# Another set of per-stage settings for the order of a fused attention and MLP kernel, without GpSimd's waits on the shared port

## The chip, the cores and the metric

The kernel runs on one core of one Trainium2 chip. The metric is the device time of one execution in microseconds, the median of three runs. Where the profile is spoken of, times are those of one profiled execution, and its span runs from the first to the last instruction of the program.

Engine names in the profile: PE is TensorE's matmul, PEld its weight load, DVE is VectorE, ACT is ScalarE, POOL is GpSimd, SP is SyncE, which issues most of the DMAs.

## The reference, cut to what matters

The input x has 2,048 rows of 512 numbers in bfloat16. Two branches work on it and a gate, one number per row, mixes them.

```python
def _A_ref(x, wqkv, wo):                       # attention: H = 32 heads of Dh = 16
    qkv = (x @ wqkv).reshape(B, S, 3, H, Dh).transpose(2, 0, 3, 1, 4)
    q, k, v = qkv[0], qkv[1], qkv[2]
    scores = jnp.einsum("bhqd,bhkd->bhqk", q, k) * (Dh ** -0.5)
    p = _softmax(scores, axis=-1)
    o = jnp.einsum("bhqk,bhkd->bhqd", p, v)
    return o.transpose(0, 2, 1, 3).reshape(B, S, D) @ wo

def _B_ref(x, w1, w2, w3, w4):                 # mixer: layernorm, w1, gelu, shifts by 1 and 2 rows, w2
    ...
    x1 = x + hs
    h2 = _gelu(_layernorm(x1, axis=-1) @ w3) @ w4   # MLP, F = 1792
    return x1 + h2

g = _sigmoid((x * gate_w).sum(-1, keepdims=True))
return g * a + (1 - g) * b
```

With 32 heads, 2,048 queries and 2,048 keys, the scores are 32 x 4 x 16 = 2,048 tiles of 128 keys x 512 queries. Each has to be exponentiated. That is the greatest part of the work.

## The kernel before

**How a score tile becomes probabilities.** There are two ways. ScalarE takes two tiles at once out of PSUM (psA), applies the exponential and writes bfloat16 into a PA buffer; each tile then needs one matmul with V, which adds into acc. VectorE takes one tile at a time (from a bank called ring), and computes the bits of a power of two directly: one multiplication and one addition, written as a 16-bit integer that is read as bfloat16. To make the approximation smooth, four copies of that integer, each shifted by a further constant, are all multiplied with V (two of them with a scaled V2) and added up. So a VectorE tile costs one first pass, a share of three shifted copies (made for two tiles at once, a pair), and four matmuls with V.

```python
def p1():                                        # VectorE, first pass, one tile
    nc.vector.tensor_scalar(out=pr["buf"].slot[:, h * 512:(h + 1) * 512], in0=buf.slot[:], scalar1=BITS_MUL,
                            scalar2=BITS_ADD, op0=ALU.mult, op1=ALU.add)
```

Who makes the three shifted copies k = 1, 2, 3 of a pair is decided when the pair is closed, by two settings and the urgency:

```python
def close_pair(pr):
    evs["n"] = evs.get("n", 0.0) + K.GP2         # every time the sum reaches 1: copy 2 too on GpSimd
    both = evs["n"] >= 1.0
    if both:
        evs["n"] -= 1.0
    rl = pr["pv"][0][0]
    alone = n_left(rl) <= (K.URG_L if rl == NR - 1 else K.URG)
    evs["m"] = evs.get("m", 0.0) + 1.0 - K.GP3   # every time the sum reaches 1: all three on VectorE
    if evs["m"] >= 1.0:
        evs["m"] -= 1.0
        alone = True
    both = both and not alone
    ...
    for k in range(1, 4):
        def sh(k=k):
            d = [b.slot for b in bufs]
            if alone or k == 1 or k == 2 and not both:
                return nc.vector.tensor_scalar(out=d[k][:, 0:w], in0=d[0][:, 0:w], scalar1=float(SHIFT * k), ...)
            return nc.gpsimd.tensor_scalar(out=d[k][:, 0:w], in0=d[0 if both else 2][:, 0:w], scalar1=1.0,
                                           scalar2=float(SHIFT * (k if both else 1)), op0=ALU.mult, op1=ALU.add)
        if alone or k == 1 or k == 2 and not both:
            j = dve(..., pr["jobs"], sh, prio=K.S_PRIO, acq=[bufs[k]], frees=[bufs[0]], port=True)
        else:
            j = gp(..., pr["jobs"] if both else last, sh, prio=1, acq=[bufs[k]], ...)   # gp() sets port=True
        ...
```

So in the ordinary case VectorE makes copies 1 and 2 from the first one, and GpSimd makes copy 3 from copy 2. There are 12 PD buffers for these integers.

**How the order comes about.** When the program is built, a small model of the engines (the class Sim) plays the whole kernel through with assumed durations and decides what each engine does next. The instructions are then issued in the order of the model's times; on the chip each engine works through its own list in that order, and semaphores keep the data right. The model treats a VectorE job and a GpSimd job that are both marked `port=True` as excluding each other:

```python
if any(not self.free[b.cls] for b in j.acq) or j.port and self.lock > self.t:
    continue
...
self.emit(self.t, self.in_port_order(e, j.fn) if j.port else j.fn)
self.t_free[e] = self.t + j.hold
if j.port:
    self.lock = self.t + j.hold
```

The kernel before carries that order over to the chip in one direction: each GpSimd instruction of such a job waits for the last VectorE instruction marked `port` that precedes it in the plan.

```python
def in_port_order(self, e, fn):
    def issue():
        inst = fn()
        if e == "DVE":
            self.last_port = inst
        elif inst is not None and self.last_port is not None:
            self.tc.add_manual_dep(inst.ins, self.last_port.ins.name, ..., reason="port")
    return issue
```

**The settings.** The model's choices depend on some two dozen settings, K. They have defaults (BASE), and for each stage of 32 score tiles (SEG = 32, so 64 stages) some of them are replaced:

```python
BASE = dict(P1_PRIO=0.414, S_PRIO=0.38, GP2=0.0, GP3=1.0, DVE_STOP=6, DVE_STOP_L=8, URG=5, URG_L=17, DVE_ALONE=2,
            EARLY=68, SL=(45, 60), IDLE_NS=537, PD_LOW=0, PA_LOW=0, DVE_WAIT=3, AHEAD=9, AHEAD2=9, PV_FULL=0.916,
            PV_IDLE=0.37, PRESS=27, MAXU=9, ROT=0, DUE_SH=0, AT_SH=0)
...
def pe_pick():
    t = sim.t
    if sim.tiles // SEG != stage[0]:
        stage[0] = sim.tiles // SEG
        K.__dict__.update({**BASE, **STAGES.get(stage[0], {})})
```

GP2 and GP3 share out the shifted copies as shown. P1_PRIO and S_PRIO rank VectorE's first passes and shifted copies. AHEAD and AHEAD2 say how far tiles of the next round may be taken early; a round is 64 tiles, one head from each of four groups, that add into acc together. DVE_ALONE and DVE_WAIT say when VectorE may be given a tile and how many may wait for it. PV_FULL, PV_IDLE, PRESS, SL, IDLE_NS and MAXU decide how many matmuls with V, and of the projections and the MLP, go between two batches of score matmuls. EARLY, AT_SH and DUE_SH shift when projections and MLP may or must run.

When a round's 64 tiles are done, VectorE copies acc out (accsb), its sums go through DRAM, are inverted and multiplied by the gate, come back broadcast (bcs), and GpSimd multiplies both into oT; this GpSimd instruction is marked `port` too, as are those of the layernorm (rs).

Of the kernel before, what the change touches and what calls it, by code (L numbers as in the profile page):

```python
# [11 lines left out]
ALU = mybir.AluOpType  # L12
# [7 lines left out]
SHIFT = 32  # L20
# [69 lines left out]
class Sim:  # L90
# [47 lines left out]
            self.n += 1  # L138
            self.order.append((t, self.n, fn))

    def in_port_order(self, e, fn):

        def issue():
            inst = fn()
            if e == "DVE":
                self.last_port = inst
            elif inst is not None and self.last_port is not None:
                self.tc.add_manual_dep(inst.ins, self.last_port.ins.name, mybir.DependencyInfo(
                    mybir.DependencyClass.Sync, mybir.DependencyReason.DATA), reason="port")
        return issue  # L150

    def finish_job(self, job):
        job.done = self.t
        self.release(job.frees)
# [1 line left out]
    def try_engine(self, e):  # L156
        if self.t_free[e] > self.t:
            return False
        best = None
        for j in self.jobs[e]:  # L160
            if j.at > self.tiles:
                continue
            if j.ready is None:
                if any(d.done is None for d in j.deps):
                    continue
                j.ready = self.t
            if any(not self.free[b.cls] for b in j.acq) or j.port and self.lock > self.t:
                continue
            key = (j.prio, j.ready, j.seq)
            if best is None or key < best[0]:  # L170
                best = (key, j)
        if best is None:
            return False
        j = best[1]
        self.jobs[e].remove(j)
        for b in j.acq:
            self.take(b)
        j.start = self.t
        self.emit(self.t, self.in_port_order(e, j.fn) if j.port else j.fn)
        self.t_free[e] = self.t + j.hold  # L180
        if j.port:
            self.lock = self.t + j.hold
        self.busy[e] += j.hold
        self.log.append((e, self.t, j.hold, j.name))
        self.push(self.t + j.hold, None)
        self.pending -= 1
        self.push(self.t + j.hold + j.lat, lambda: self.finish_job(j))
        return True
# [57 lines left out]
def kernel(  # L246
# [14 lines left out]
    nc = tc.nc  # L261
# [35 lines left out]
        P1_PRIO=0.414,  # L297
        S_PRIO=0.38,
        GP2=0.0,
        GP3=1.0,  # L300
        DVE_STOP=6,
        DVE_STOP_L=8,
        URG=5,
        URG_L=17,
        DVE_ALONE=2,
        EARLY=68,
        SL=(45, 60),
        IDLE_NS=537,
        PD_LOW=0,
        PA_LOW=0,  # L310
        DVE_WAIT=3,
        AHEAD=9,
        AHEAD2=9,
        PV_FULL=0.916,
        PV_IDLE=0.37,
# [2 lines left out]
        ROT=0, DUE_SH=0, AT_SH=0,  # L318
    )
    SEG = 32  # L320
    STAGES = {0: {'AHEAD': 6, 'EARLY': 13, 'DVE_ALONE': 150, 'S_PRIO': 0.368}, 1: {'AHEAD': 8, 'S_PRIO': 0.415}, 2: {'ROT': 3, 'URG': 3, 'MAXU': 9, 'PD_LOW': 3}, 3: {'PA_LOW': 3, 'DVE_WAIT': 4}, 4: {'SL': (25, 60), 'URG': 2, 'DVE_STOP_L': 9, 'DUE_SH': 40}, 5: {'SL': (25, 60), 'URG': 2, 'DVE_STOP_L': 9, 'DUE_SH': 40}, 6: {'S_PRIO': 0.234}, 7: {'PRESS': 17, 'DVE_WAIT': 5}, 8: {'PV_FULL': 0.776, 'AHEAD': 7, 'PD_LOW': 0}, 9: {'PV_FULL': 0.877, 'ROT': 2, 'AHEAD': 6, 'PA_LOW': 0}, 10: {'PV_FULL': 0.794, 'PA_LOW': 0, 'SL': (165, 60), 'DVE_ALONE': 2}, 11: {'SL': (85, 100), 'EARLY': 62}, 12: {'EARLY': 124, 'PV_IDLE': 0.433, 'DVE_STOP_L': 11, 'SL': (25, 40)}, 13: {'GP3': 0.6, 'DVE_ALONE': 150}, 14: {'ROT': 3, 'GP3': 0.9, 'URG_L': 16, 'AHEAD2': 12}, 15: {'P1_PRIO': 0.309, 'DVE_STOP_L': 5, 'AT_SH': 60, 'DVE_STOP': 5}, 16: {'DVE_WAIT': 2, 'AHEAD2': 10}, 17: {'ROT': 1, 'AT_SH': 10, 'GP3': 0.8, 'DVE_ALONE': 2}, 18: {'P1_PRIO': 0.403, 'GP2': 0.2}, 19: {'PRESS': 10}, 20: {'URG': 7, 'AT_SH': 60, 'GP2': 0.2}, 21: {'IDLE_NS': 352, 'DVE_ALONE': 300}, 22: {'S_PRIO': 0.257}, 23: {'PRESS': 52, 'AT_SH': 60}, 24: {'PA_LOW': 3, 'PRESS': 23, 'GP3': 0.8}, 25: {'PV_IDLE': 0.414, 'AT_SH': 10}, 26: {'DUE_SH': 8, 'PD_LOW': 1, 'GP2': 0.2, 'GP3': 0.9}, 28: {'AHEAD2': 10, 'EARLY': 142}, 29: {'AHEAD': 8, 'S_PRIO': 0.388, 'GP3': 0.9, 'ROT': 1}, 30: {'PV_IDLE': 0.372, 'DUE_SH': -40, 'S_PRIO': 0.412, 'PA_LOW': 2}, 31: {'IDLE_NS': 311, 'GP3': 0.9, 'P1_PRIO': 0.22}, 32: {'DUE_SH': 40, 'DVE_STOP': 5}, 33: {'DVE_STOP_L': 7, 'SL': (205, 60)}, 34: {'P1_PRIO': 0.326, 'PD_LOW': 0, 'PV_IDLE': 0.37, 'GP2': 0.35}, 36: {'PD_LOW': 1, 'DVE_STOP': 7}, 37: {'URG': 4, 'IDLE_NS': 589}, 38: {'ROT': 2}, 39: {'EARLY': 155, 'PA_LOW': 3}, 40: {'DUE_SH': -20, 'PRESS': 8}, 41: {'P1_PRIO': 0.584, 'PA_LOW': 3, 'MAXU': 10}, 42: {'AHEAD2': 8, 'PRESS': 58, 'DVE_ALONE': 0}, 43: {'PD_LOW': 0, 'DVE_WAIT': 2, 'P1_PRIO': 0.216, 'PV_FULL': 1}, 44: {'MAXU': 7, 'ROT': 1}, 45: {'PRESS': 10, 'SL': (65, 80)}, 46: {'DVE_WAIT': 6, 'AT_SH': 120, 'PD_LOW': 0}, 47: {'DUE_SH': 80, 'P1_PRIO': 0.59, 'DVE_ALONE': 150, 'AHEAD2': 6}, 48: {'URG': 8, 'AT_SH': 120}, 49: {'PD_LOW': 3, 'ROT': 3, 'DVE_WAIT': 6, 'AT_SH': 120}, 50: {'DVE_WAIT': 1, 'SL': (5, 60), 'GP2': 0.35, 'DVE_STOP_L': 11}, 51: {'PA_LOW': 3, 'URG_L': 18}, 52: {'ROT': 2, 'PD_LOW': 1, 'PRESS': 35}, 53: {'URG_L': 16, 'IDLE_NS': 245, 'PRESS': 19}, 54: {'PD_LOW': 3}, 56: {'MAXU': 10, 'GP2': 0.1}, 57: {'URG': 2}, 58: {'ROT': 3, 'DVE_WAIT': 5}, 59: {'ROT': 1}, 60: {'GP2': 0.2, 'PV_FULL': 0.879, 'SL': (85, 100)}, 61: {'GP3': 0.6, 'GP2': 0.35, 'PV_FULL': 0.985}, 62: {'GP3': 0.6, 'GP2': 0.35, 'PV_FULL': 0.985}}
    K = SimpleNamespace(**BASE)


# [70 lines left out]
        "den": slots("den", 3, [4, 512], F32, dpool),  # L395
        "rr": slots("rr", 3, [4, 512], F32, dpool),
    })
    sim.tc = tc
    sim.last_port = None

    def dve(hold, deps, fn, **kw):
        return sim.add(Job("DVE", hold, 280.0, deps, fn, **kw))
# [558 lines left out]
    def close_pair(pr):  # L961
        evs["pair"] = None
        evs["n"] = evs.get("n", 0.0) + K.GP2
# [5 lines that stand above are left out]
        evs["m"] = evs.get("m", 0.0) + 1.0 - K.GP3  # L969
# [4 lines that stand above are left out]
        w = 512 * pr["h"]  # L974
        bufs = [pr["buf"]] + [Buf("PD", pr["h"] + (k == 2)) for k in range(1, 4)]
        pr["buf"].users = pr["h"] + (3 if both or alone else 2)
        bufs[2].users = pr["h"] + (0 if both or alone else 1)
        last = list(pr["jobs"])
        chain = [last]
        for k in range(1, 4):  # L980
            def sh(k=k):
                d = [b.slot for b in bufs]
                if alone or k == 1 or k == 2 and not both:
                    return nc.vector.tensor_scalar(out=d[k][:, 0:w], in0=d[0][:, 0:w], scalar1=float(SHIFT * k),  # L984
                                                   scalar2=None, op0=ALU.add)
                return nc.gpsimd.tensor_scalar(out=d[k][:, 0:w], in0=d[0 if both else 2][:, 0:w], scalar1=1.0,  # L986
                                               scalar2=float(SHIFT * (k if both else 1)), op0=ALU.mult, op1=ALU.add)
            if alone or k == 1 or k == 2 and not both:
                j = dve(0.26 * w + 72.0, pr["jobs"], sh, prio=K.S_PRIO, acq=[bufs[k]], frees=[bufs[0]], port=True)
            else:  # L990
                j = gp(0.833 * w + 165.0, pr["jobs"] if both else last, sh, prio=1, acq=[bufs[k]],
                       frees=[bufs[0 if both else 2]])
            if k == 3:
                j.frees.append(pr["token"])
            last = [j]
            chain.append(last)
        for h2, (r2, kt2, i2, G2, p2) in enumerate(pr["pv"]):
            for k in range(4):
                hd = 8 * G2 + 2 * i2 + p2
                V = (lambda kt=kt2, hd=hd: V0[:, kt, hd, :]) if k < 2 else (lambda kt=kt2, hd=hd: V2[:, kt // 2, hd, :])  # L1000
                add_pv(r2, i2, kt2, V, lambda h2=h2, b=bufs[k]: b.slot[:, h2 * 512:(h2 + 1) * 512].bitcast(BF16),
                       list(chain[k]) + [j_v[kt2, G2 // 2] if k < 2 else j_v2[kt2, G2 // 2]], bufs[k])
# [371 lines left out]
```

The softmax here doesn't subtract the row's maximum and nothing guards it: scores larger than these inputs give would overflow.

## Time and profile before

| what | value |
|---|---|
| time, median of 3 runs (lowest to highest) | 772.39 us (772.31 to 772.64) |
| span of the profiled execution | 770.4 us, at a granted TensorE clock of 1.00 |
| instructions | 23,725 |
| score tiles on ScalarE, on VectorE | 1,483 and 565 |
| shifted copies on VectorE, on GpSimd | 579 and 270 |

In the profile's groups a row names the line, engine and operation, what is written and read, the shapes and the count; then the busy time and the mean duration of one; then how long the engine was idle just before such instructions, and what ended most of that idle time. A mean longer than busy time divided by the count says that neighbours overlap: the exponential shows a mean of 1,052 ns, but 742 of them fill only 689.8 us. In the list of waits a row gives who waited, for whom, the total, the number of times and the longest, in us. The line numbers: L922 is the exponential, L948 VectorE's first pass, L984 and L986 the shifted copies on VectorE and GpSimd, L842 the score matmul, L1017 the matmul with V, L532 the projections and the MLP, L1050 GpSimd's oT, L603, L623, L695 and L753 other VectorE instructions marked `port`, L684 the layernorm's on GpSimd.

### The profile page before, as it was taken

Reading aid. Unit: us, or ns where it says so; the run is one execution under the profiler, and the core shown is the slowest. Engines: PE = TensorE matmul, PEld = TensorE weight load, DVE = VectorE, ACT = ScalarE, POOL = GpSimd, SP = SyncE. Lnnn points to the kernel's source line nnn. Section 1 sums busy time; section 2 is a strip of 40 time slices with the busy share of each in tenths; the row PEclk is TensorE's granted clock in tenths of the full one; section 3 lists DMA queues with packets and bytes.
Section 4 is the critical chain, followed back from the end, with each engine's and each line's share of the span. In section 5 each row is a group of like instructions: output and inputs, shape, how many; then the busy total and the mean of one; then the engine's idle time right before and its main releaser. Section 6 shows DMA issues by size and latency. Waiting matters only on the chain.

```text
span 770.4 us, 23725 instructions
## 1 busy us (share of the span) xinstructions
PE 758.7 (98%) x9588; PEld 227.8 (30%) x9588; DVE 725.2 (94%) x1575; ACT 739.7 (96%) x767; POOL 335.2 (44%) x332
## 2 busy tenths in 40 slices
PE   9999999999999999999999999999999999999997
PEld 5333322223222222233232224222233222223222
DVE  6999999999999999998989998999999889999996
ACT  6899999999999999999989999999999999999995
POOL 2345533443344444344345553344454454454531
PEclk9999999999999999999999999999999999999999
DMA  9402133122001221141001001001100000000001
GB/s 192 142 3 35 54 98 88 47 72 89 6 19 34 61 72 46 48 125 50 17 18 33 23 20 47 23 27 27 41 19 19 23 19 22 27 20 20 13 18 38
DMA packets 67093, 34.60 MB, mean 45 GB/s; under 512 B 46748, under 2 KB 62380, under 8 KB 66984
## 3 DMA queue, kind: packets, MB, share of 16 engines
q1 hardware_dynamic: 66040, 32.56, 16.3%
q8 instruction: 75, 1.23, 0.6%
q10 hardware_dynamic: 944, 0.52, 0.2%
q14 instruction: 34, 0.28, 0.1%
HBM read 17.40 MB, written 6.81 MB: 31 GB/s over the span
## 4 chain that ended last, share of the span: by engine, by line
PE 71%; ACT 22%; DVE 4%; issue 3%; ACTq 0%; DVEq 0%
PE acc L1017 26%; PE psA L842 23%; PE ring L532 20%; ACT PA L922 16%; DVE PD L948 2%; ACT hT L766 2%; ACT hB L766 2%; DVE PD L984 1%; ACT hT L735 1%; ACT L922 1%; PE ring L842 1%; PE ring L510 0%; ACT L766 0%; PE ring L1295 0%; DVE hB L765 0%
## 5 line engine op out<-in xcount | busy, mean ns | idle before, releaser
L922 ACT ACTIVATE PA<-psA 128x1024 bf16<-128x1024 f32 x742 | 689.8, 1052 | 16.8 <-PE acc L1017 7.7
L986 POOL TENSOR_SCALAR PD<-PD 128x1024 uint16<-128x1024 uint16 x270 | 281.8, 1048 | 384.7 <-DVE PD L984 215.8
L948 DVE TENSOR_SCALAR PD<-ring 128x512 uint16<-128x512 f32 x565 | 372.9, 680 | 25.9 <-PE ring L842 23.6
L1017 PE MATMUL acc<-PD,V 128*17 128x512 bf16 x2260 | 307.3, 381 | 1.0 <-DVE accsb L1033 0.8
L842 PE MATMUL psA<-q,kT 32*128 32x512 bf16 x1483 | 285.8, 384 | 5.3 <-ACT PA L922 4.4
L1017 PE MATMUL acc<-PA,V 128*17 128x512 bf16 x1483 | 277.6, 381 | 0.0
L984 DVE TENSOR_SCALAR PD<-PD 128x1024 uint16<-128x1024 uint16 x579 | 226.2, 429 | 1.5 <-PE acc L1017 0.8
L842 PE MATMUL ring<-q,kT 32*128 32x512 bf16 x565 | 190.7, 384 | 0.0
L842 PEld LDWEIGHTS <-kT 32*128 32x128 bf16 x2048 | 76.8, 91 | 311.0 <-issue 309.0
L1017 PEld LDWEIGHTS <-V 128*17 128x17 bf16 x3743 | 74.9, 88 | 129.1 <-issue 107.0
L532 PE MATMUL ring<-xnT,w 128*32 128x512 bf16 x1152 | 89.0, 382 | 0.0
L532 PE MATMUL ring<-w,hT 128*32 128x512 bf16 x704 | 58.5, 383 | 0.1
L532 PEld LDWEIGHTS <-w 128*32 128x32 bf16 x1920 | 45.2, 95 | 43.9 <-issue 30.3
L1050 POOL TENSOR_TENSOR oT<-accsb,bcs 128x512 bf16<-128x512 f32 x31 | 39.5, 1275 | 24.7 <-DVE PD L984 19.4
L532 PE MATMUL ring<-w,w 128*32 128x256 bf16 (+1 forms) x768 | 41.1, 311 | 0.0
L532 PE MATMUL ring<-w,hB 128*32 128x512 bf16 x448 | 36.0, 383 | 0.0
L1033 DVE COPY accsb<-acc 128x512 f32<-128x512 f32 x31 | 21.1, 681 | 1.1 <-PE acc L1017 1.0
L675 DVE BATCH_NORM_STATS2 st<-x_sb 128x6 f32<-128x512 bf16 x32 | 21.5, 678 | 0.0
L532 PE MATMUL ring<-w,wq 128*32 128x512 bf16 x256 | 21.2, 383 | 0.2 <-ACT w L561 0.2
L532 PEld LDWEIGHTS <-hT 128*32 128x32 bf16 x704 | 14.8, 95 | 20.3 <-issue 15.5
L765 DVE CAST hT<-ring 128x512 bf16<-128x512 f32 x28 | 18.8, 680 | 1.1 <-PE ring L532 0.9
L765 DVE CAST hB<-ring 128x512 bf16<-128x512 f32 x28 | 19.0, 682 | 0.9 <-PE ring L532 0.7
(93 smaller groups left out, 263.5 us busy)
## 6 DMA issues: line engine op xcount, KB each, us to landing
bcs<-rr SPq DMA_DIRECT2D x124, 64.0 KB
xn_dram<-xn SPq DMA_DIRECT2D x32, 128.0 KB
w<-in_B_w_dram SPq DMA_DIRECT2D x5, 512.0 KB
oD<-oT SPq DMA_DIRECT2D x124, 16.0 KB
w<-in_B_w_dram SPq DMA_DIRECT2D x4, 448.0 KB
out_dram<-ot SPq DMA_DIRECT2D x14, 128.0 KB
x_sb<-in_A_x_dram SPq DMA_DIRECT2D x3, 512.0 KB
w<-in_A_wqkv_dram SPq DMA_DIRECT2D x2, 256.0 KB
```

What stands on the lines that cost most here:

```text
L532: units.append([Op("col", j, lambda j=j, lf=lf, rf=rf, n0=n0, n1=n1, st=st, sp=sp: nc.tensor.matmul(get()[32 * j:32 * j + 32, n0:n1], lhsT ...
L675: a = dve(600, deps, lambda: nc.vector.bn_stats(out=sb.slot[:], in_=x_sb[:, t, :]), prio=6, at=at, acq=[sb])
L765: pre.append(evac(g, PSUM_NS, lambda ps, m=m: nc.vector.tensor_copy(out=h2()[:, m, :], in_=ps[:])))
L766: ge = act(93 + 427 * FT + 2600, pre, lambda: nc.scalar.activation(out=h2(), in_=h2(), func=ACT.Gelu_apprx_tanh), prio=0)
L842: o = Op("row", i, lambda: nc.tensor.matmul(dst(), lhsT=kT[G][32 * i:32 * i + 32, kt * P:(kt + 1) * P], rhs=qbuf[G, c].slot[32 * i:32 * i ...
L922: job = act(hold, ops, lambda: nc.scalar.activation(out=pb.slot[:, 0:n], in_=buf.slot[:, 0:n], func=ACT.Exp, scale=0.25), acq=[pb], frees= ...
L948: nc.vector.tensor_scalar(out=pr["buf"].slot[:, h * 512:(h + 1) * 512], in0=buf.slot[:], scalar1=BITS_MUL, scalar2=BITS_ADD, op0=ALU.mult, ...
L984: return nc.vector.tensor_scalar(out=d[k][:, 0:w], in0=d[0][:, 0:w], scalar1=float(SHIFT * k), scalar2=None, op0=ALU.add)
L986: return nc.gpsimd.tensor_scalar(out=d[k][:, 0:w], in0=d[0 if both else 2][:, 0:w], scalar1=1.0, scalar2=float(SHIFT * (k if both else 1)) ...
L1017: o = Op("col", i, lambda: nc.tensor.matmul(acc[32 * i:32 * i + DH + 1, :], lhsT=lhs(), rhs=rhs(), start=st, stop=True, tile_position=(0, ...
L1033: e = dve(PSUM_NS, round_ops[r], lambda: nc.vector.tensor_copy(out=ab.slot[:], in_=acc[:]), acq=[ab], prio=0)
L1050: n = gp(1250, d3, lambda: nc.gpsimd.tensor_tensor(out=ob.slot[:], in0=ab.slot[:], in1=bb.slot[:], op=ALU.mult), acq=[ob], frees=[ab, bb], ...
```

## The change

The method in_port_order and its use are taken out, so GpSimd waits for its data and buffers only. The table STAGES is replaced by another one, from a search that judged each stage's settings by a longer stretch of what follows. Nothing else is changed: the defaults, the model of the engines, the buffers and all instructions that can be chosen are the same. The purpose is an order in which the engines are idle less.

```diff
             self.order.append((t, self.n, fn))
-
-    def in_port_order(self, e, fn):
-
-        def issue():
-            inst = fn()
-            if e == "DVE":
-                self.last_port = inst
-            elif inst is not None and self.last_port is not None:
-                self.tc.add_manual_dep(inst.ins, self.last_port.ins.name, mybir.DependencyInfo(
-                    mybir.DependencyClass.Sync, mybir.DependencyReason.DATA), reason="port")
-        return issue
 
...
-        self.emit(self.t, self.in_port_order(e, j.fn) if j.port else j.fn)
+        self.emit(self.t, j.fn)
...
-    STAGES = {0: {'AHEAD': 6, 'EARLY': 13, 'DVE_ALONE': 150, 'S_PRIO': 0.368}, 1: {'AHEAD': 8, 'S_PRIO': 0.415}, 2: {'ROT': 3, 'URG': 3, 'MAXU': 9, 'PD_LOW': 3}, 3: {'PA_LOW': 3, 'DVE_WAIT': 4},
-          ... (stages 4 to 62: 57 more entries, as the kernel before has them)
+    STAGES = {0: {'DVE_ALONE': 150}, 1: {'GP2': 0.35, 'PRESS': 12, 'SL': (5, 60)},
+              2: {'P1_PRIO': 0.391, 'DUE_SH': 80, 'URG': 7}, 3: {'URG_L': 19, 'GP2': 0.35}, 4: {'GP2': 0.2},
+              5: {'SL': (65, 80)}, 6: {'P1_PRIO': 0.23, 'DVE_ALONE': 2, 'SL': (25, 40), 'EARLY': 4},
+              7: {'AT_SH': 10, 'DVE_STOP': 4, 'GP2': 0.35, 'P1_PRIO': 0.249},
+              8: {'GP2': 0.2, 'PV_FULL': 0.941, 'IDLE_NS': 755}, 9: {'SL': (5, 20), 'EARLY': 113, 'PV_IDLE': 0.548},
+              10: {'GP2': 0.2}, 11: {'SL': (165, 180)}, 12: {'PV_FULL': 0.802, 'DUE_SH': 20}, 13: {'S_PRIO': 0.554},
+              14: {'PV_FULL': 0.752, 'SL': (85, 100)}, 15: {'IDLE_NS': 519, 'PA_LOW': 0, 'URG_L': 19, 'GP2': 0.2},
+              16: {'EARLY': 155, 'DUE_SH': 40}, 17: {'GP2': 0.35, 'PD_LOW': 3}, 18: {'GP2': 0.35, 'MAXU': 11},
+              19: {'S_PRIO': 0.349, 'ROT': 1, 'GP3': 0.8}, 20: {'ROT': 1, 'DVE_STOP': 8, 'DVE_ALONE': 0, 'GP3': 0.8},
+              21: {'DVE_WAIT': 5, 'PRESS': 8}, 22: {'PD_LOW': 1, 'ROT': 3, 'DVE_STOP_L': 10, 'SL': (85, 60)},
+              23: {'URG_L': 20, 'URG': 7, 'AT_SH': 120}, 24: {'IDLE_NS': 835, 'ROT': 2, 'DVE_ALONE': 150},
+              25: {'DVE_ALONE': 300}, 26: {'DVE_ALONE': 500, 'PV_FULL': 0.937, 'IDLE_NS': 716},
+              27: {'DVE_STOP': 4, 'GP2': 0.2, 'PV_FULL': 0.781, 'DVE_STOP_L': 9},
+              28: {'AT_SH': 120, 'PV_FULL': 0.847, 'DUE_SH': 8}, 29: {'URG': 4, 'GP3': 0.8, 'DVE_ALONE': 150},
+              30: {'PA_LOW': 2, 'PD_LOW': 0, 'PV_FULL': 0.79, 'GP2': 0.2}, 31: {'ROT': 1}, 32: {'SL': (205, 220)},
+              33: {'SL': (205, 220), 'AHEAD2': 11, 'PV_IDLE': 0.391}, 34: {'S_PRIO': 0.546}, 35: {'ROT': 2, 'URG': 8},
+              36: {'IDLE_NS': 401, 'P1_PRIO': 0.419}, 37: {'GP2': 0.1}, 38: {'AHEAD2': 12, 'AT_SH': 30, 'ROT': 3},
+              39: {'IDLE_NS': 301, 'URG_L': 14, 'AT_SH': 120}, 40: {'GP2': 0.1, 'AHEAD2': 11, 'EARLY': 63, 'S_PRIO': 0.549},
+              41: {'GP2': 0.35, 'EARLY': 58, 'PA_LOW': 0}, 42: {'PA_LOW': 3}, 43: {'PRESS': 10, 'DVE_ALONE': 2},
+              44: {'ROT': 2}, 45: {'GP3': 0.6, 'S_PRIO': 0.381, 'AT_SH': 30}, 46: {'AT_SH': 120},
+              47: {'PRESS': 13, 'AT_SH': 10, 'URG': 8, 'S_PRIO': 0.248}, 49: {'AT_SH': 120, 'DVE_STOP': 7, 'EARLY': 71},
+              50: {'PA_LOW': 0, 'AHEAD2': 11, 'DVE_ALONE': 300, 'PD_LOW': 0}, 51: {'GP2': 0.35, 'S_PRIO': 0.435},
+              52: {'SL': (85, 60)}, 53: {'DVE_STOP': 7, 'PD_LOW': 2, 'GP2': 0.35},
+              54: {'GP3': 0.9, 'AT_SH': 120, 'SL': (65, 60), 'P1_PRIO': 0.31}, 55: {'PA_LOW': 1, 'ROT': 1},
+              56: {'GP2': 0.35, 'PA_LOW': 0}, 57: {'P1_PRIO': 0.451, 'DVE_WAIT': 2, 'SL': (65, 80), 'DVE_ALONE': 2},
+              58: {'PV_IDLE': 0.477, 'SL': (165, 180), 'PD_LOW': 1}, 59: {'DVE_ALONE': 300},
+              60: {'S_PRIO': 0.595, 'GP3': 0.8, 'DVE_STOP': 3, 'AHEAD': 6}, 61: {'PRESS': 11, 'PV_IDLE': 0.427},
+              62: {'DVE_STOP_L': 7, 'AHEAD': 10, 'EARLY': 125, 'SL': (65, 80)},
+              63: {'PA_LOW': 0, 'SL': (25, 60), 'DVE_STOP_L': 6}, 64: {'AHEAD': 7, 'DVE_WAIT': 1, 'SL': (85, 100)}}
...
-    sim.tc = tc
-    sim.last_port = None
... (in close_pair, sh() no longer returns its instruction)
```

The settings that share out the shifted copies, stage by stage (default GP2 = 0, GP3 = 1):

| | GP2 | GP3 |
|---|---|---|
| before | 0.2 in 18, 20, 26, 60; 0.35 in 34, 50, 61, 62; 0.1 in 56 | 0.6 in 13, 61, 62; 0.8 in 17, 24; 0.9 in 14, 26, 29, 31 |
| after | 0.35 in 1, 3, 7, 17, 18, 41, 51, 53, 56; 0.2 in 4, 8, 10, 15, 27, 30; 0.1 in 37, 40 | 0.8 in 19, 20, 29, 60; 0.6 in 45; 0.9 in 54 |

## The prediction

> **What bounds the kernel now.** I read the page's busy shares first, then busy time by stretch, then the waits, then the chain. The busy shares:
>
> ```profile
> PE 758.7 (98%) x9588; PEld 227.8 (30%) x9588; DVE 725.2 (94%) x1575; ACT 739.7 (96%) x767; POOL 335.2 (44%) x332
> ```
>
> Three engines look full. PE's 98% can't be taken as a limit: the matmuls overlap (one shows 381 ns, four neighbours start together) and the weight loads fill only 30%. ScalarE and VectorE are occupied one instruction at a time, so theirs is the better measure. The cost of one score tile on each comes from the groups:
>
> ```profile
> L922 ACT ACTIVATE PA<-psA 128x1024 bf16<-128x1024 f32 x742 | 689.8, 1052 | 16.8 <-PE acc L1017 7.7
> L986 POOL TENSOR_SCALAR PD<-PD 128x1024 uint16<-128x1024 uint16 x270 | 281.8, 1048 | 384.7 <-DVE PD L984 215.8
> L948 DVE TENSOR_SCALAR PD<-ring 128x512 uint16<-128x512 f32 x565 | 372.9, 680 | 25.9 <-PE ring L842 23.6
> ...
> L984 DVE TENSOR_SCALAR PD<-PD 128x1024 uint16<-128x1024 uint16 x579 | 226.2, 429 | 1.5 <-PE acc L1017 0.8
> ```
>
> ScalarE takes 1,483 of the 2,048 tiles, two in one instruction: 689.8 / 1,483 = 0.465 us a tile. VectorE takes 565: 372.9 / 565 = 0.66 us for the first pass, and 226.2 / 565 = 0.40 us for its share of the shifted copies, 1.06 us in all. GpSimd makes 270 copies and idles for more than half of the span. Now the stretches (us, then busy time of PE, PEld, DVE, ACT, POOL; then clock and DMA):
>
> ```profile
> 0.00:25.00 25.00, 23.48 (x359) 11.96 (x359) 17.52 (x40) 17.60 (x22) 7.02 (x17) 1.00 1.00 221
> 25.00:50.00 25.00, 25.00 (x371) 9.27 (x367) 24.99 (x58) 22.38 (x25) 9.43 (x9) 1.00 0.13 38
> 50.00:350.00 300.00, 297.49 (x3671) 86.96 (x3664) 295.48 (x674) 297.80 (x312) 129.92 (x128) 1.00 0.22 58
> 350.00:750.00 400.00, 396.47 (x5010) 114.77 (x5009) 373.85 (x778) 389.48 (x398) 185.10 (x175) 1.00 0.09 24
> 750.00:771.00 21.00, 16.23 (x192) 4.79 (x189) 13.39 (x29) 12.47 (x15) 3.75 (x4) 0.98 0.13 42
> ```
>
> From 50 to 350 us ScalarE is idle for 2.2 us and VectorE for 4.5: nothing is to be had there except by moving work to GpSimd. From 350 to 750 ScalarE is idle for 10.5 us and VectorE for 26.2: there a better order has something to find. The ramps hold another 10 us of idle ScalarE before 50 us and some 8 after 750. The chain that ended last agrees only in part: most of it is matmuls, and most of its longest pieces are runs of ScalarE's exponentials between them.
>
> ```profile
> PE 71%; ACT 22%; DVE 4%; issue 3%; ACTq 0%; DVEq 0%
> ```
>
> So the kernel is bound by **ScalarE's and VectorE's work together**, with some 31 us of VectorE's and 13 us of ScalarE's idle time, between 50 and 750 us, as what can be won; the end follows whichever ran out of work or fell behind.
>
> **What the Trainium skill says.** "SBUF — State Buffer", section "Who interferes with whom": VectorE's second port pair is GpSimd's only one, it is an exclusive lock held for a whole instruction, and whoever issues first blocks the other. A tensor_scalar from SBUF to SBUF in a two-port mode takes it. The trace agrees: the shifted copy on VectorE has a minimum, median and maximum of 286/417/1262 ns, and each of its long ones lies beside a GpSimd instruction that had started first. An example, VectorE and then GpSimd in the same microseconds:
>
> ```profile
> 425.92 1.10 DVE L984 TENSOR_SCALAR PD<-PD 128x1024 uint16<-128x1024 uint16 x2
> ```
> ```profile
> 424.35 2.06 POOL L986 TENSOR_SCALAR PD<-PD 128x1024 uint16<-128x1024 uint16 x2 [1.18 <-DVE PD L984]
> ```
>
> Two copies that take 0.75 us elsewhere took 1.10 here, because the second GpSimd copy held on until 426.41. The Trainium skill's "Perfetto Trace Analysis", section "Identifying the Most-Contended Engine", says that the matmul row is a poor measure and occupancy a fair one for the other engines; that is how I read the first line above.
>
> **The change, part by part.**
>
> *1. The waits go.* In the kernel before, every GpSimd job that the plan marks as using the port waits for VectorE's last port instruction ahead of it. How much is that worth to GpSimd? Most of its idle time ends with its own operand: a third copy on GpSimd reads the second copy, which VectorE makes, so the 215.8 us "PD L986 <- DVE PD L984" is largely a data wait and stays. What can only be the port wait are the waits of instructions whose data don't come from the releaser:
>
> ```profile
> POOL oT L1050 <- DVE PD L984: 19.4, 15, 3.5
> ...
> POOL PD L986 <- DVE q L603: 8.1, 4, 2.2
> POOL PD L986 <- DVE xn L695: 4.9, 3, 1.8
> ...
> POOL rs L684 <- DVE xn L695: 4.2, 2, 3.1
> POOL rs L684 <- DVE PD L984: 3.5, 3, 1.5
> ```
>
> That is 40.1 us over 27 waits; with the small ones (L623, L753, and the reciprocal-side lines) I take 45 us and 32 waits. GpSimd has 435 us of idle time, so its own time gains nothing at the end. Copies may reach the matmuls up to 1.5 us earlier, which frees some of the 12 PD buffers sooner; VectorE shows under 2 us of idle time ahead of its copies, so those buffers aren't what it waits for. Gain: about 0.
>
> *2. What the waits kept away may come back.* Collisions cost VectorE now (429 - 417) x 579 = 7 us in all. Without the waits, GpSimd can start first where the plan wanted VectorE first. If half of the 32 foreign waits turn into collisions, at half a GpSimd copy (0.52 us) each, VectorE loses 16 x 0.52 = 8 us. From 350 us on it has idle time to absorb part of it; before 350 it has none. I charge a quarter to a third to the end: **+2 to +3 us**.
>
> *3. GpSimd gets more copies.* GP2 is the share of pairs whose second copy also goes to GpSimd, 1 - GP3 the share whose third goes back to VectorE. Summed over the stages that set them, GP2 rises from 2.3 to 4.55, and 1 - GP3 falls from 2.0 to 1.3. There are 283 pairs in 64 stages, 4.4 a stage: (2.25 + 0.7) x 4.4 = 13 copies leave VectorE. Back to back, one costs it 0.33 us (three took 1.08 us at 423.12, so (1.08 - 0.417) / 2): 4.3 us. VectorE can then take more tiles: x tiles more cost it 1.06x and relieve ScalarE of 0.465x; equal relief at 4.3 - 1.06x = 0.465x, x = 2.8, worth 1.3 us to both. **-1.3 us**, expected as about 566 shifted copies on VectorE and 283 on GpSimd, at an unchanged number of pairs.
>
> *4. All other settings change.* None of the 64 entries equals its predecessor; 160 values instead of 161, over the same 24 names, with the same defaults. They decide which matmuls go into PE's gaps, when VectorE takes a score tile alone, how far ahead of the round tiles may be taken. No instruction gets cheaper. What it can win is idle time: the 12.7 us of ScalarE and 30.7 us of VectorE from 50 to 750 us (from the table), plus a little of the ramps. If both were filled completely, moving x tiles to VectorE with 30.7 = 1.06x gives 29 tiles or 13 us of ScalarE, and its own 12.7 us come on top: 26 us is the ceiling. The order before has been chosen in the same way, stage by stage, so I expect a new choice with a longer view to find a sixth of it, **-4 us**, with a wide margin both ways: a plan that looks better need not be, once the chip's durations drift from it.
>
> Sum: 772.4 + 2.5 - 1.3 - 4 = 769.6, rounded to **769.5 us**.
>
> **The rivals.**
>
> *The lost waits cost more than the settings bring.* Where GpSimd runs out of step with the plan, every copy on VectorE can be caught behind a 1.05 us instruction. If 60 copies more are caught, VectorE loses 31 us; before 350 us it is at 98%, so half would reach the end: 780 to 785 us. For it: VectorE's copies are paired, so one delay holds the second too, and more GP2 pairs put two GpSimd copies in a row. Against it: today's collisions (7 us) happen with the waits in place, so the waits are only part of what keeps the engines apart; the data order does most.
>
> *VectorE isn't the limit after 350 us, PE is.* There PE shows no gaps while both others idle (10.5 and 26.2 us). A VectorE tile costs four value matmuls where a ScalarE tile costs one (2,260 = 4 x 565). If PE's order is what holds that stage, more VectorE tiles slow it, and only better packing helps: between 766 and 774 us, whatever happens to GpSimd.
>
> *The search pays in full.* A third of the 26 us and no new collisions: 762 us. For it: the new entries reach stages 63 and 64, the drain, where the old ones stop at 62. Against it: ScalarE has 2.2 us of idle time in the whole of 50 to 350 us.
>
> **Range and chances.** Two orders of the same work, both tuned, should lie within a few us; the terms above are uncertain by about 3 us for the collisions and 6 for the settings, together some 7, so 8 in 10 is 760 to 779 us. Two per cent is 15.4 us: faster needs under 757, nearly the ceiling of 26 us; slower needs over 788, more than the first rival's. Chances: faster 0.04, same 0.92, slower 0.04. That it is faster at all I hold for 6 in 10.
>
> **What would show it.** Step 1: "oT <- DVE PD L984" (19.4 us) shrinks to a few us, the span doesn't follow. Step 2: the mean of VectorE's copy over its 417 ns median; 429 becomes about 443 if I am right, over 470 if the first rival is. Step 3: copies of about 566 on VectorE and 283 on GpSimd, and 1,475 to 1,490 tiles on ScalarE. Step 4: idle time of ScalarE between 350 and 750 us, 10.5 now, about 7 then. The prediction is wrong if ScalarE's tile count moves by more than 20, if the ramps shift by more than 3 us, or if copies on VectorE average over 470 ns.

## The result, and the profile after

The changed kernel takes **785.12 us** (783.33 to 787.05 over 4 runs) against 772.37 us (772.31 to 772.64): a ratio of 1.0165, 95% interval 1.0139 to 1.0191. It is 12.7 us slower, outside the predicted range, and its runs lie 3.7 us apart where those of the kernel before lie within 0.3 us (within 1.6 us in a later set of 21 runs). (Line numbers are 13 or 12 lower after: L909 is the exponential, L935 the first pass, L971 and L974 the shifted copies on VectorE and GpSimd, L1038 GpSimd's oT.)

The busy shares of the changed kernel:

```profile
PE 766.3 (98%) x9650; PEld 228.1 (29%) x9650; DVE 741.9 (95%) x1560; ACT 744.8 (95%) x766; POOL 361.5 (46%) x352
```

VectorE has 15 instructions fewer than before (1,560 instead of 1,575) and is busy 16.7 us longer (741.9 instead of 725.2). The groups of the changed kernel say which instructions grew:

```profile
L909 ACT ACTIVATE PA<-psA 128x1024 bf16<-128x1024 f32 x741 | 694.9, 1038 | 23.0 <-PE psA L829 9.0
L974 POOL TENSOR_SCALAR PD<-PD 128x1024 uint16<-128x1024 uint16 x290 | 306.5, 1062 | 391.4 <-DVE PD L971 248.4
L935 DVE TENSOR_SCALAR PD<-ring 128x512 uint16<-128x512 f32 x567 | 371.0, 678 | 18.3 <-PE ring L829 16.8
...
L971 DVE TENSOR_SCALAR PD<-PD 128x1024 uint16<-128x1024 uint16 x562 | 235.9, 457 | 1.6 <-PE acc L1005 0.5
```

The first pass is the same as before (678 and 680 ns). The shifted copy has a mean of 457 ns instead of 429, although its median is 415 (before: 417): 17 copies fewer took 9.7 us more. The chain of the changed kernel, and two stretches of it:

```profile
PE 54%; DVE 28%; ACT 10%; issue 4%; DMA 2%; SPq 1%; DVEq 0%; ACTq 0%
```
```profile
50.00:350.00 300.00, 295.22 (x3610) 84.65 (x3602) 295.89 (x642) 293.60 (x308) 145.40 (x141) 1.00 0.20 52
350.00:750.00 400.00, 394.57 (x4997) 114.34 (x4995) 378.25 (x767) 387.34 (x389) 188.50 (x175) 1.00 0.11 29
```

VectorE's share of the chain has gone from 4% to 28%. From 50 to 350 us VectorE is as busy as before (295.9 us) with 642 instructions instead of 674, and ScalarE's idle time has tripled, from 2.2 to 6.4 us: it now waits for VectorE there, by way of PE. What ends ScalarE's waits is PE in both kernels; new is that PE's matmuls with V wait for VectorE's copies (before, then after):

```profile
L1017 PE MATMUL acc<-PD,V 128*17 128x512 bf16 x2260 | 307.3, 381 | 1.0 <-DVE accsb L1033 0.8
```
```profile
L1005 PE MATMUL acc<-PD,V 128*17 128x512 bf16 x2268 | 301.2, 381 | 2.5 <-DVE PD L971 2.0
```

Of these 2.0 us 1.2 are there with the new settings alone; with the old settings and no waits it is 2.2 us (both versions follow below). This shows the path of the delay, not all of its size.

In what follows, **held time** is a sum over VectorE's instructions in the trace: what each took above the median of its own kind, where that is more than 60 ns. It was 9.8 us in 24 instructions before, and is 32.9 us in 44 after, about a quarter of it in VectorE instructions other than the shifted copies.

### The profile page after: what moved, and what is told of

It is laid out like the page before. It is cut to its first block, busy times and chain, and to the rows that moved or that the text cites. A ratio compares the mean times of both kernels' runs of the same rounds, so it can differ in the third digit from the quotient of the medians.

```text
span 782.1 us, 23875 instructions
## 1 busy us (share of the span) xinstructions
PE 766.3 (98%) x9650; PEld 228.1 (29%) x9650; DVE 741.9 (95%) x1560; ACT 744.8 (95%) x766; POOL 361.5 (46%) x352
## 4 chain that ended last, share of the span: by engine, by line
PE 54%; DVE 28%; ACT 10%; issue 4%; DMA 2%; SPq 1%; DVEq 0%; ACTq 0%
PE acc L1005 19%; PE psA L829 17%; PE ring L519 16%; DVE PD L935 11%; DVE PD L971 9%; ACT PA L909 6%; ACT hT L753 2%; DVE st L662 1%; DMA pk<-den 1%; DVE x_sb L731 1%; DVE xn L682 1%; ACT hT L722 1%; DMA xn_dram<-xn 1%; DVE hT L752 1%; PE ring L829 1%
## 5 line engine op out<-in xcount | busy, mean ns | idle before, releaser
L909 ACT ACTIVATE PA<-psA 128x1024 bf16<-128x1024 f32 x741 | 694.9, 1038 | 23.0 <-PE psA L829 9.0
L974 POOL TENSOR_SCALAR PD<-PD 128x1024 uint16<-128x1024 uint16 x290 | 306.5, 1062 | 391.4 <-DVE PD L971 248.4
L935 DVE TENSOR_SCALAR PD<-ring 128x512 uint16<-128x512 f32 x567 | 371.0, 678 | 18.3 <-PE ring L829 16.8
L1005 PE MATMUL acc<-PD,V 128*17 128x512 bf16 x2268 | 301.2, 381 | 2.5 <-DVE PD L971 2.0
L1005 PE MATMUL acc<-PA,V 128*17 128x512 bf16 x1481 | 273.0, 381 | 0.0
L971 DVE TENSOR_SCALAR PD<-PD 128x1024 uint16<-128x1024 uint16 x562 | 235.9, 457 | 1.6 <-PE acc L1005 0.5
L829 PE MATMUL ring<-q,kT 32*128 32x512 bf16 x567 | 193.0, 384 | 2.4 <-DVE PD L935 1.3
L829 PEld LDWEIGHTS <-kT 32*128 32x128 bf16 x2048 | 74.6, 91 | 305.4 <-issue 304.2
L519 PE MATMUL ring<-xnT,w 128*32 128x512 bf16 x1152 | 92.0, 383 | 0.8 <-DVE qf L588 0.2
L1038 POOL TENSOR_TENSOR oT<-accsb,bcs 128x512 bf16<-128x512 f32 x31 | 40.8, 1316 | 7.5 <-DMA bcs<-rr 7.1
L519 PE MATMUL ring<-wo,oD 128*32 128x512 bf16 x224 | 19.8, 384 | 0.0
L519 PE MATMUL ring<-w,wq 128*32 128x512 bf16 x256 | 19.0, 386 | 0.2 <-DVE hT L752 0.2
```

Of the source, the lines that this page charges most:

```text
L519: units.append([Op("col", j, lambda j=j, lf=lf, rf=rf, n0=n0, n1=n1, st=st, sp=sp: nc.tensor.matmul(get()[32 * j:32 * j + 32, n0:n1], lhsT ...
L829: o = Op("row", i, lambda: nc.tensor.matmul(dst(), lhsT=kT[G][32 * i:32 * i + 32, kt * P:(kt + 1) * P], rhs=qbuf[G, c].slot[32 * i:32 * i ...
L909: job = act(hold, ops, lambda: nc.scalar.activation(out=pb.slot[:, 0:n], in_=buf.slot[:, 0:n], func=ACT.Exp, scale=0.25), acq=[pb], frees= ...
L1005: o = Op("col", i, lambda: nc.tensor.matmul(acc[32 * i:32 * i + DH + 1, :], lhsT=lhs(), rhs=rhs(), start=st, stop=True, tile_position=(0, ...
L1038: n = gp(1250, d3, lambda: nc.gpsimd.tensor_tensor(out=ob.slot[:], in0=ab.slot[:], in1=bb.slot[:], op=ALU.mult), acq=[ob], frees=[ab, bb], ...
```

## The experiments

Theory 1: without the waits GpSimd starts just ahead of VectorE, and VectorE is held until GpSimd is done. Theory 2: the new settings give a worse order. Theory 3: the 20 copies that GpSimd makes more do it.

| kernel | us, median (range) | held us (instructions) |
|---|---|---|
| before (old settings, waits) | medians from 772.05 to 772.52 in the four sets of runs beside the experiments | 9.8 (24) |
| old settings, no waits | 783.30 (782.21 to 785.31) | 28.9 (42) |
| new settings, waits | 773.50 (772.11 to 777.19) | 11.7 (25) |
| after (new settings, no waits) | 785.12 (783.33 to 787.05) | 32.9 (44) |
| new settings, no waits, copies in halves | 783.78 (783.01 to 784.41) | 31.8 (82) |
| old settings, waits, copies in halves | 773.88 (773.55 to 775.24) | 16.3 (94) |
| old settings, waits on copies only | 776.14 (775.89 to 777.02) | 19.4 (36) |
| old settings, waits on the others only | 777.79 (777.20 to 778.79) | 19.5 (36) |
| old settings, no waits, quarter copies | 782.20 (782.12 to 782.74) | 9.7 (31) |
| old settings, waits, quarter copies | 781.37 (781.24 to 781.40) | 0.3 (3) |
| old settings, waits, GpSimd yields in the plan | 786.46 (785.43 to 787.13) | 11.0 (24) |
| old settings, waits both ways | 775.04 (774.78 to 776.50) | 0 (0) |
| default settings, waits | 813.40 (813.12 to 813.92) | 14.6 (34) |
| default settings, no waits | 824.06 (823.55 to 825.19) | 31.0 (46) |

### The two halves of the change, one at a time

```diff
 # the changed kernel, the table STAGES of the kernel before
-    STAGES = {0: {'DVE_ALONE': 150}, 1: {'GP2': 0.35, ...
+    STAGES = {0: {'AHEAD': 6, 'EARLY': 13, ...
```

> The settings of the kernel before, without the port waits: half of the change alone. Theory 1 (without the waits GpSimd starts first and VectorE is held by the lock): 779 to 786 us, the mean of VectorE's shifted copy rises from 429 ns to 445 ns or more, and runs spread by several us as in the changed kernel (783.3 to 787.1). Theory 2 (the new settings give a worse order by themselves): 772 us give or take 1.5, mean copy 425 to 435 ns. Theory 3 (it is the 20 more copies on GpSimd that block VectorE): 772 to 775 us.

Measured: 783.3 us, ratio 1.0138 (1.0121 to 1.0155).

```diff
 # the kernel before, the table STAGES of the changed one
-    STAGES = {0: {'AHEAD': 6, 'EARLY': 13, ...
+    STAGES = {0: {'DVE_ALONE': 150}, 1: {'GP2': 0.35, ...
```

> The new settings with the port waits put back: the other half alone. Theory 1: 767 to 774 us, mean copy on VectorE about 430 ns, runs within 1 us of each other. Theory 2: 783 to 787 us although the mean copy is back at 430 ns. Theory 3: 776 to 782 us, mean copy still 440 ns or more, since a wait holds GpSimd back but nothing holds VectorE back.

Measured: 773.5 us, ratio 1.0021 (1.0010 to 1.0031). The group of VectorE's copy in these two kernels, without waits and with them:

```profile
L971 DVE TENSOR_SCALAR PD<-PD 128x1024 uint16<-128x1024 uint16 x579 | 240.6, 453 | 1.1 <-PE acc L1005 0.2
```
```profile
L984 DVE TENSOR_SCALAR PD<-PD 128x1024 uint16<-128x1024 uint16 x562 | 222.1, 433 | 1.6 <-PE acc L1017 0.5
```

The waits make nearly all of the difference, 10.8 us (783.30 - 772.49); theories 2 and 3 fall as its cause. With the waits the new settings, 20 more GpSimd copies included, cost 1.0 us (773.50 - 772.49); without the waits the old settings lose nearly as much as the new. One expectation missed: the new settings with waits spread over 5 us, not 1. Why isn't settled, but the clock goes with it in part: of the seven runs above 774 us five show a mean granted clock of 0.995 to 0.997, and every other run 0.999 or 1.0.

What a lost wait looks like can be seen in these two kernels with the old settings, since they have the same plan. Kernel before, VectorE and then GpSimd (start, length, count):

```profile
196.40 1.09 DVE L984 TENSOR_SCALAR PD<-PD 128x1024 uint16<-128x1024 uint16 x3
```
```profile
197.66 1.05 POOL L986 TENSOR_SCALAR PD<-PD 128x1024 uint16<-128x1024 uint16 x1 [2.40 <-DVE PD L984]
```

The same instructions without the waits:

```profile
201.10 1.93 DVE L971 TENSOR_SCALAR PD<-PD 128x1024 uint16<-128x1024 uint16 x3
```
```profile
201.70 1.06 POOL L974 TENSOR_SCALAR PD<-PD 128x1024 uint16<-128x1024 uint16 x1 [1.78 <-DVE PD L971]
```

VectorE makes three copies in a row, 0.33 us apart. GpSimd's operand is the first of them: it ends at 201.10 + 0.42 = 201.52, and GpSimd starts 0.18 us later, at 201.70. VectorE's third copy would start at 201.10 + 2 x 0.33 = 201.77, 0.07 us too late, and is held by GpSimd's, which ends at 202.76: the three take 1.93 us instead of 1.09. The wait was on the third copy; with it GpSimd starts 1.26 us after the first instead of 0.60, and nobody needs its result sooner: in the kernel before no engine waited for any of GpSimd's 270 copies. Such a near tie comes about again and again: of the 33 VectorE copies above 500 ns in this run, 13 had a GpSimd copy start 65 to 105 ns ahead of them and took about 1.26 us (in the kernel before, one of 21). In 12 of the others it was oT that held them, up to a length of 1.50 us.

The two kernels have the same 1,575 VectorE instructions in the same order, so the holds can be matched one by one. Without the waits 33 instructions are held that weren't before, for 25.4 us in all or 0.77 us each: 19 by a shifted copy on GpSimd, 13 by oT, one by another instruction. Of the 24 held before, 15 no longer are. And for 9 of the 19 it is as in the example: in the kernel before that GpSimd copy had stood idle and started 0.15 to 0.19 us after the end of the very VectorE copy that it now holds.

### Shorter holds, in two ways

GpSimd's copies in two instructions of half the width, in the changed kernel and (first half waiting) in the kernel before:

```diff
-nc.gpsimd.tensor_scalar(out=d[k][:, 0:w], in0=d[...][:, 0:w], ...)
+for a in range(0, w, w // 2):
+    nc.gpsimd.tensor_scalar(out=d[k][:, a:a + w // 2], in0=d[...][:, a:a + w // 2], ...)
```

> The changed kernel with each of GpSimd's shifted copies made as two instructions of half the width, same data, same plan. Theory 1: a blocked VectorE copy waits for the rest of one half only, so its excess over the median falls from 33 us in all to 15 to 20 us and the time to 776 to 781 us, although GpSimd works longer. Theory 2: 784 to 787 us, since the order is the same. If the number of collisions doubles as their length halves: no change in time, 785 us.

> The kernel before (waits, old settings) with GpSimd's copies in two halves, the first of which waits. Theory 1: the excess of VectorE's port instructions falls from 10 us to about 5 us and the time to 769 to 772 us. Against it: GpSimd's copies end later by the fixed cost of one instruction more, so their matmuls come later: 772 to 775 us.

Measured: 783.8 and 773.9 us. The copies of the changed kernel in halves, GpSimd's and VectorE's groups:

```profile
L975 POOL TENSOR_SCALAR PD<-PD 128x512 uint16<-128x512 uint16 x580 | 353.7, 630 | 347.9 <-DVE PD L971 215.3
...
L971 DVE TENSOR_SCALAR PD<-PD 128x1024 uint16<-128x1024 uint16 x562 | 236.4, 458 | 1.6 <-PE acc L1007 0.5
```

What theory 1 expected of both failed: the held time stayed at 31.8 us in the one and rose from 9.8 to 16.3 us in the other. A single hold is half as long (0.39 instead of 0.75 us on average), but there are twice as many, 82 instead of 44: a half takes 0.61 us, so GpSimd is busy for longer in all (353.7 us instead of 306.5), and each half can hold another copy. In the changed kernel the case named for that, no change in time, is what came; in the kernel before the time lies in the range named against theory 1. So these two runs don't tell the lock from something else; a hold that is shorter in total is needed.

```diff
 # old settings, without and with waits; three quarters of GpSimd's copies are left out
-nc.gpsimd.tensor_scalar(out=d[k][:, 0:w], in0=d[...][:, 0:w], ...)
+nc.gpsimd.tensor_scalar(out=d[k][:, 0:w // 4], in0=d[...][:, 0:w // 4], ...)
...
+for s_ in list(sim.free["PD"]):       # the 12 buffers are filled once, early
+    sim.emit(1500.0, lambda s_=s_: nc.vector.memset(s_[:, 128:1024], 16256.0))
```

> The old settings without waits, same plan, but each GpSimd copy writes only the first quarter of its columns (three quarters of that copy are left out of the computation; the buffers are filled with a constant once at the start, while VectorE would idle, which may cost up to 1 us). GpSimd's hold falls from 1.05 us to about 0.3 us, while who starts first stays as it is. Lock theory: the excess on VectorE falls from 29 us to 10 to 14 us, what is left being mostly oT, and the time to 774 to 777 us. If the waits help by when the copies arrive or by the order of the matmuls, and not through the lock: 781 to 785 us.

> The fourth corner of a square of waits (with, without) and hold (whole copy, a quarter): old settings, waits on, GpSimd copies a quarter wide, the same fill of the buffers at the start as in the run without waits. That fill turned out to delay everything by some 9 us, so this run is to be compared with the run without waits and quarter copies (782.2) alone. Lock theory: the waits are worth 11 us with whole copies and at most 2 us with quarter copies: 780 to 782.5 us. If the waits work in another way: 770 to 773 us, 11 us less than without them.

Measured: 782.2 us without and 781.4 us with waits. A quarter copy takes 0.41 us instead of 1.05, not the 0.3 that I had expected. The fill was misjudged: it took VectorE 11.15 us ahead of its first work, so both start some 9 us late and their times can't be set against 772 us. Two readings need no such comparison. The first is the pair itself: the waits are worth **0.8 us with quarter copies and 10.8 us with whole ones** (783.3 - 772.5); the 0.8 is no firmer than the 0.5 us between the medians of the kernel before in these two sets of runs. The second is the stretch from the first to the last start of VectorE's shifted copy, from the line of that instruction (minimum, median, maximum in ns; first and last start in us). Before; no waits; quarter copies without waits; quarter copies with waits:

```profile
L984 DVE TENSOR_SCALAR PD<-PD x579: 286/417/1262, 12.7 to 759.8; 128x1024 uint16<-128x1024 uint16 x192, 128x512 uint16<-128x512 uint16 x1
```
```profile
L971 DVE TENSOR_SCALAR PD<-PD x579: 284/415/1504, 12.4 to 772.8; 128x1024 uint16<-128x1024 uint16 x192, 128x512 uint16<-128x512 uint16 x1
```
```profile
L971 DVE TENSOR_SCALAR PD<-PD x579: 286/416/1465, 21.6 to 769.7; 128x1024 uint16<-128x1024 uint16 x192, 128x512 uint16<-128x512 uint16 x1
```
```profile
L984 DVE TENSOR_SCALAR PD<-PD x579: 284/418/541, 22.0 to 768.7; 128x1024 uint16<-128x1024 uint16 x192, 128x512 uint16<-128x512 uint16 x1
```

That makes 747.1, 760.4, 748.1 and 746.7 us. Shortening what GpSimd holds, with the order left as it is, takes away 12.3 of the 13.3 us that the waits were worth (in these executions; the one without waits and with whole copies is the slowest of its four). So the waits work through the time for which GpSimd holds VectorE, and not through when the copies come. The first and the last of these lines also show that the 9.8 us held in the kernel before cost nothing: with waits, 0.3 us held gives 746.7 and 9.8 us held 747.1. Those holds are in the plan, which reserves the time for them; the 19 us on top aren't. One thing stays open: without waits but with quarter copies oT, whose width is unchanged, still held VectorE for 6.0 of the 9.7 us, and all that cost at most 1.4 us. So what a held microsecond costs depends on what else is held; these runs don't show how.

### Which waits

The waits on the shifted copies alone, and on the other GpSimd instructions (oT, the layernorm) alone:

```diff
-self.emit(self.t, self.in_port_order(e, j.fn) if j.port else j.fn)
+self.emit(self.t, self.in_port_order(e, j.fn) if j.port and (e == "DVE" or j.name == "copy") else j.fn)
 # and the other: j.name != "copy"
```

> The old settings; only GpSimd's shifted copies keep the port wait, the 31 multiplications into oT and the layernorm's small instructions lose it. In the run without any wait about 8 of the 33 longest VectorE copies lay beside an oT multiplication, at about 1.07 us each, the rest beside a copy. Lock theory, cost in proportion to the blocked time: 774 to 777 us, about 8 us more excess on VectorE than with all waits. If only the copies matter: 772 to 773 us.

> The old settings; only the oT multiplications and the small instructions keep the wait, the 270 copies lose it. Lock theory: 778 to 782 us, excess on VectorE about 20 us, nearly all of it in copies of about 1.26 us (0.417 and the 0.845 left of a GpSimd copy that started just ahead). If only oT matters: 772 to 774 us.

Measured: 776.1 us (ratio 1.0053, 1.0038 to 1.0068) and 777.8 us (1.0073, 1.0058 to 1.0088). Both parts count: losing the waits of oT and the layernorm costs 3.6 us, losing those of the copies 5.3, together 8.9 of the 10.8. In the first of the two runs oT holds VectorE for 10.1 us and the layernorm's instructions for none, so the 3.6 us go to the 31 oT multiplications, a tenth of GpSimd's instructions. The held time of both is 19.4 and 19.5 us, halfway between 9.8 and 28.9.

### Does it hang on the settings, and what are they worth?

```diff
-    STAGES = {0: {...}, 1: {...}, ...}
+    STAGES = {}          # with the waits, and without them
```

> No stage settings at all, the defaults throughout, with the port waits. What the choice by stage is worth, on the chip: if the settings are mostly noise to the chip, 772 to 777 us; if the search carries over, 785 to 800 us. I lean to about 783 us.

> The defaults throughout, without the waits. Lock theory: the waits' worth doesn't hang on the settings, so 8 to 14 us above the defaults with waits, and the excess of VectorE's port instructions 15 to 25 us above that run's. If the loss belongs to the two tuned tables, which were fitted tightly to a plan that knows the lock: less than 5 us.

Measured: 813.4 and 824.1 us. The waits are worth 10.7 us here, 10.8 with the old settings and 11.6 with the new: it doesn't hang on the table. And the settings by stage are worth 41 us on the chip, far more than I leaned to; the two tables differ by 1.0 us of that. Part of the 41, and of the 10.7, may be the clock's: from 50 to 350 us it was granted at 0.98 with the defaults and waits and at 0.97 without, at 1.00 in the kernel before.

### Two attempts to go further

GpSimd gives way in the plan, too: there it doesn't start a port job while VectorE is about to be free and has one ready.

```diff
+            if e == "POOL" and j.port and self.t_free["DVE"] < self.t + 150.0 and any(
+                    x.port and ... for x in self.jobs["DVE"]):
+                continue
```

> Old settings with all waits, and the model of the engines doesn't start a GpSimd port job while VectorE is free within 150 ns and has a port job ready: GpSimd yields in the plan, too, and the waits carry it over. Lock theory: the 10 us of excess left in the kernel before fall to 5 us or less; if the plan is otherwise as good, 768 to 772 us. The settings were chosen for the other plan, so a worse order could cost more than that: up to 778 us.

Measured: 786.5 us. The held time didn't fall (11.0 us), and VectorE is idle for 47 us between 50 and 750 us instead of 31. This is another plan, for which neither table was chosen; with settings chosen for it, it wasn't tried.

The plan's port order in both directions:

```diff
             if e == "DVE":
                 self.last_port = inst
+                if inst is not None and self.last_pool is not None:
+                    self.tc.add_manual_dep(inst.ins, self.last_pool.ins.name, ..., reason="port")
             elif inst is not None and self.last_port is not None:
...
+            if e != "DVE" and inst is not None:
+                self.last_pool = inst
```

> The old settings with the port order of the plan enforced in both directions: VectorE's port instructions wait for GpSimd's last one ahead of them in the plan, too. Lock theory: VectorE would be held by the lock in those places anyhow, so the time lost only changes its name, from long copies to idle time: excess on VectorE about 0 instead of 10 us, its idle time some 10 us more, and 771.5 to 774 us. If the order GpSimd first were often broken on the chip to VectorE's advantage, the second wait costs: 775 to 780 us.

Measured: 775.0 us, ratio 1.0037 (1.0024 to 1.0051). The group of VectorE's copy:

```profile
L989 DVE TENSOR_SCALAR PD<-PD 128x1024 uint16<-128x1024 uint16 x579 | 219.0, 417 | 16.7 <-POOL PD L991 11.8 <-POOL oT L1055 1.3 <-PE acc L1022 0.2
```

No copy is held any longer (mean 417 ns), but the idle time ahead of the copies has risen from 1.5 to 16.7 us. Elsewhere it fell, so VectorE's idle time between 50 and 750 us rose from 30.7 to 38.1 us, by less than the 9.8 us of holds that are gone. What the 2.5 us (775.04 - 772.52) are lost to isn't shown; the time lies at the edge of the range named for the case that the chip often broke the order GpSimd first to VectorE's advantage. Here only the direction GpSimd-after-VectorE was worth a wait. No version here beats the kernel before.

## Why the prediction was wrong, step by step

**What bounds the kernel: right as far as it went.** Holding VectorE longer made the kernel longer, and its share of the chain rose from 4% to 28%; PE still makes up 54% of it.

**Step 1, the waits gone: right about GpSimd, and that hid the point.** I sorted the waits by what they cost GpSimd, 45 us of an engine with 435 us idle, and concluded that they matter to nobody. The wait of oT for VectorE's copies (19.4 us) is gone, as expected. What is left of oT's waits in the changed kernel is for its data:

```profile
POOL oT L1038 <- DMA bcs<-rr: 7.1, 4, 3.9
```

**Step 2, the collisions: this is the step that failed, a mis-sized term.** I put it at +2 to +3 us; with the plan kept it measured +10.8 us. The mechanism was the one that I named, GpSimd starting first where the plan wanted VectorE first, but all three factors were too small.

- The number: 16 new holds expected, 33 found (15 old ones went). I had counted only waits whose data can't come from the releaser, and set the 215.8 us of "PD L986 <- DVE PD L984" aside as waits for data. But the port wait hides in that row, too: GpSimd's operand is one VectorE copy and the port wait is for a later one, as in the example and for 9 of the new holds.
- The length: half a GpSimd copy, 0.52 us, as if GpSimd's start fell anywhere; measured 25.4 / 33 = 0.77 us, because GpSimd often starts just ahead of VectorE and holds it for most of its length, and because oT is longer. The Trainium skill's "SBUF — State Buffer", section "Who interferes with whom", says that whoever issues first gets the shared ports for the whole instruction. That allows a hold of nearly a whole instruction; the average of a half was my own assumption. The trace agrees with the page: 13 copies were held for about 0.845 us by a GpSimd copy of 1.05.
- The share that reaches the end: a quarter to a third; measured 10.8 / 19.1 = 0.57, where 19.1 is 28.9 - 9.8, the holds gained less those gone (by the spans of the two profiled executions, 13.1 / 19.1 = 0.69). I had read VectorE's 31 us of idle time as slack. It absorbed less than half of the 19.1: each engine has a fixed list, and a late copy delays PE and ScalarE before the next gap comes. Between 50 and 750 us VectorE's idle time fell only from 30.7 to 26.4 us, and ScalarE's rose from 12.7 to 20.1.

**Step 3, more copies on GpSimd: counts right, gain not seen.** 562 copies on VectorE and 290 on GpSimd (566 and 283 predicted), 1,481 tiles on ScalarE. With waits, VectorE's busy time fell by 1.9 us, and the time rose by 1.0.

**Step 4, the settings: wrong in sign, small in size.** The run with the waits measures steps 3 and 4 together: -5.3 us predicted, +1.0 us measured. ScalarE's idle time from 350 to 750 us, which was to fall from 10.5 to about 7 us, is 9.9 us there and 12.7 in the changed kernel. This other choice of settings found nothing in the idle time.

**The rivals.** The first came closest, with "780 to 785 us" and half of the lost time reaching the end, but partly by luck: it expected 60 more holds of 0.52 us, and 33 new ones of 0.77 us came. The test for it, a mean copy above 470 ns, was set too high: 457 ns was enough, and it leaves out what other instructions were held. The second rival asked for no effect of GpSimd at all, and the third for a gain; both fall.

## What to carry to other kernels

Where two engines exclude each other, a wait on the engine with idle time can protect the one without: judge such a wait by what it keeps from the busy engine, not by how long the idle one stands in it. A dependency that isn't needed for the data may still hold up the plan's order, so when order and waits are changed together, measure each alone. And when a statically ordered engine is late, take its idle time as slack only where the trace shows that lateness being absorbed.

## What the runs showed of the hardware that I had not expected

Near ties fall the wrong way with regularity: without the waits GpSimd started 65 to 105 ns ahead of a VectorE copy 13 times, and the copy then took about 1.26 us instead of 0.42. Halving GpSimd's instructions didn't help (31.8 us held instead of 32.9), since a half still takes 0.61 us of the 1.05. The changed kernel's runs are also less even (783.3 to 787.1 us), but that isn't tied to the waits: the new settings with waits spread from 772.1 to 777.2 us.
